# Two heads in one unit of the 64-row chunks of an attention and expert kernel, sums from a column of ones, and a new order

## The chip, the cores and the metric

The kernel runs on one core of a Trainium2 chip. The time is that of one execution on the device, in microseconds. PE is TensorE, PEld its weight load, DVE VectorE, ACT ScalarE, POOL GpSimd, SP SyncE, whose queue issues most of the DMA transfers here.

## What is computed

```python
B, H, S, D = q.shape                      # 4, 8, 576, 64
scores = scale * np.matmul(q, k.transpose(0, 1, 3, 2))
x = (psi_rel / psi_i)[..., None]          # of the two positions alone
h = np.maximum(x @ w1 + b1, 0.0)          # 32 hidden
bias = h @ w2                             # 8 heads
scores = scores + bias.transpose(2, 0, 1)[None, :, :, :]
scores = scores - np.max(scores, axis=-1, keepdims=True)
attn = np.exp(scores)
attn = attn / (np.sum(attn, axis=-1, keepdims=True) + 1e-09)
return np.matmul(attn, v).astype(np.float32)
...
logits = xn @ en.T / tau                  # 2304 tokens, 8 experts, of the attention's output x
expert_idx = np.argmax(logits, axis=1)
gate_w = probs[np.arange(N), expert_idx]
h = np.maximum(x[mask] @ w1[e], 0.0)      # 512 to 1024
out[mask] = gate_w[mask, None] * (h @ w2[e])
```

## The kernel before, in words

The four batches are taken in two pairs `pr`. A chunk (pr, c) with c < 4 holds 128 query rows of each of the two batches; the chunk c = 4 holds the last 64 rows of both. The order is `CHUNKS`: (0, 4), (0, 0) to (0, 3), (1, 0) to (1, 3), (1, 4). A unit (`unit`, L658) is a chunk and a head, 80 in all; units 0 to 7 and 72 to 79 are those of c = 4.

A unit loads its bias `bt` from DRAM (SP, L671), multiplies Q by K on PE (L694, each product as three f16 products), adds the bias and finds the minimum on DVE (L708), takes the exponential on ACT, which also gives the row sums (L711), transposes 128x128 blocks on PE (L725), evicts them to `pts` (ACT or DVE, L731) and multiplies by V on PE (L748). Every second head DVE makes `ri` of the sums (L755, L756) and normalises into `xt` (L762, or L764 for c = 4). A full unit (c < 4) has two batches, whose QK lie in two row tiles of the array (rows 0 to 63 and 64 to 127) and in two PSUM buffers `s0` and `s1`; it has two L708, two L711, nine transposes. A unit of c = 4 has 64 rows of each batch: QK lies in two diagonal tiles (batch b in rows and columns from 64 b on), both write `s0`, and it has one L708, one L711 and five transposes; POOL copies 64 columns of `pp` (L716), so that the last transpose holds both batches.

Beside the units run: `prep_k` (per pair and four heads: raw K in `kr`, of which there is one buffer; the maxima L492 and L494, a transpose L495, L496, L497, the scale and `aq`, L483 to L489; two f16 halves `khl` by ACT and by DVE, L519; ten transposes a head on PE into `s1`, L527, and their eviction `kt`, L530); `prep_q` (L559 and L567 on POOL, L566 on DVE, then a transposing DMA `qt`, L581, since it needs `aq`); and `bias_step` (L583: `hid` on DVE, L617, a product in four column tiles, L632, `stg`, L639 or L643, and a store to DRAM, L654), which makes the bias of a chunk ahead of its units.

When a chunk's eight heads are done, `finish` (L789) normalises the rows, takes logits (L878 to L880), the best expert and gate (L884 to L893) and the rank of each token (L909 to L924). Behind the chunk (1, 3) `early_slots` (L936) fixes the first slots of the experts, behind the last chunk the tokens are gathered and the experts run (`moe`). In units 72 to 79 dummy matmuls of 512 columns (L770) stand between the work of PE.

The order of the work of attention is fixed when the program is built: `Sched` (L123) takes each operation with its engine, an estimated duration and a priority (the unit's number plus an offset such as `oS`, `oB` or `oP`, from the tables at L39 to L97), and lays one fixed row of instructions for each engine. `s1`, `m`, `t0`, `t1` and `o` are one PSUM buffer each; `s1` is shared by QK of batch 1, the K transposes and the dummies.

Of the kernel before, what the change touches and what calls it, by code (L numbers as in the profile page):

```python
# [14 lines left out]
ALU = mybir.AluOpType  # L15
# [35 lines left out]
BBK = 8  # L51
KBS = 12
KA = 19
KB = 27
QA = 13
VA = 39
KLA = 7.607
KLB = 2.85
KHB = 2.886
KP0 = 4.157  # L60
KP1 = 0.138
KH = 2.263
QL1 = 32.538
QL0 = 70.547
BL1 = 14.005
BS1 = 1.189
BP0 = -8.343
PSB = 0
ALPHA = 22.407
# [3 lines left out]
PRLD = 86.205  # L73
AVD, AVD4 = 1315, 732
# [6 lines left out]
PREP = 86.458  # L81
# [182 lines left out]
class Kern:  # L264
# [393 lines left out]
    def unit(self, u):  # L658
# [60 lines left out]
        parts = [("t0", 0, 0, 4, [0])] + ([("t1", 640, 4, 4, [1])] if c < 4 else []) + [("m", 512, 8, 1, [0, 1])]  # L719
# [851 lines left out]
```

## Time and profile before

| | before |
|---|---|
| runs, us | 641.57, 645.21, 650.35 (median 645.21) |
| profiled execution, us | 642.66, its span 640.8 |
| PE busy | 587.6 us (92%) |
| PEld | 397.0 us (62%) |
| DVE | 511.1 us (80%) |
| ACT | 466.9 us (73%) |
| POOL | 159.1 us (25%) |
| mean granted TensorE clock | 0.974 of 2.4 GHz |
| DMA | 119.98 MB, of them 93.43 MB on SP's queue |

Busy shares are means over the whole span. What bounds the kernel differs by stage: the start with the first chunk of 64 rows (0 to 82.8 us), the full chunks (to 348.4), the last chunk of 64 rows (to 373), the gather (to 406), the experts (to 606) and the last scatter.

### The profile page before, as it was taken

The page shows a single profiled execution, that of the slowest core. Times are in us where ns is not written, and L with a number is a line of the kernel's source. Part 1 is how long each engine was busy: PE and PEld are TensorE (multiplying, and loading weights), DVE is VectorE, ACT ScalarE, POOL GpSimd, SP SyncE. Part 2 cuts the span into 40 slices and gives each one's busy share as a digit, 9 for nine tenths or more (in the row PEclk, how much of TensorE's full clock was granted, in tenths as well). Part 3 has the DMA queues.
Part 4 walks back from the last instruction along what each step waited for, and adds up shares of the span by engine and source line. Part 5 has one row for each costly group of instructions (what it writes and reads, how often), then busy time and mean ns, then how long its engine had stood idle before and what let it go on. Part 6 is the DMA issues. An engine that isn't in the chain of part 4 may idle for free.

```text
span 640.8 us, 20769 instructions
## 1 busy us (share of the span) xinstructions
PE 587.6 (92%) x7647; PEld 397.0 (62%) x7647; DVE 511.1 (80%) x1426; ACT 466.9 (73%) x995; POOL 159.1 (25%) x233
## 2 busy tenths in 40 slices
PE   8677899999999889999899988789999999999993
PEld 3233556666877677787787656674576468447741
DVE  8878789899888698888987773887778887987752
ACT  6567679797989798999999543778787667758400
POOL 4454665342021044231202145200000000000173
PEclk9787899999999989999999999899999999999998
DMA  8799988579987948987988459985599479749652
GB/s 186 214 250 206 270 226 187 145 198 229 200 232 98 216 124 164 208 180 176 192 194 182 104 149 304 216 165 144 153 222 230 153 184 216 207 163 208 93 205 97
DMA packets 172027, 119.98 MB, mean 187 GB/s; under 512 B 126327, under 2 KB 147063, under 8 KB 171922
## 3 DMA queue, kind: packets, MB, share of 16 engines
q1 hardware_dynamic: 164706, 93.43, 65.4%
q0 software_dynamic: 7216, 25.14, 13.1%
q8 instruction: 67, 1.10, 0.7%
q14 instruction: 38, 0.31, 0.2%
HBM read 77.24 MB, written 21.87 MB: 155 GB/s over the span
## 4 chain that ended last, share of the span: by engine, by line
issue 35%; PE 30%; DVE 8%; POOL 4%; ACT 4%; DMA 2%; SPq 1%; POOLq 0%; DVEq 0%; ACTq 0%
PE o L748 10%; PE t L725 7%; PE s L694 7%; POOL out L1393 3%; DVE ss L708 2%; DMA macc<-xs,kept 2%; PE m L632 2%; ACT pp L711 1%; PE m L725 1%; DVE khl L519 1%; ACT pts L731 1%; POOL macc L1404 1%; PE s L770 1%; DVE hid L617 1%; DMA kr<-in_k 1%
## 5 line engine op out<-in xcount | busy, mean ns | idle before, releaser
L711 ACT ACTIVATE pp<-ss,mx 128x576 f32<-128x576 f32 x144 | 112.1, 789 | 16.7 <-DVE mx L708 11.7
L708 DVE CUSTOM_DVE_ANT_0 ss<-s,bt 128x576 f32<-128x576 f32 x144 | 104.1, 752 | 15.6 <-PE s L694 13.0
L748 PE MATMUL o<-v,pts 128*64 128x64 f32 x2880 | 103.7, 227 | 0.4 <-DVE xt L762 0.4
L748 PEld LDWEIGHTS o<-v,pts 128*64 128x64 f32 x2880 | 92.5, 140 | 13.9 <-issue 9.0
L1388 PE MATMUL p<-w2s,mht 128*128 (+1 forms) x432 | 97.4, 379 | 0.7 <-DVE macc L1488 0.4
L1388 PE MATMUL p<-w1s,mxt 128*128 (+1 forms) x768 | 96.6, 273 | 0.1
L725 PE MATMUL t<-ident,pp 128*128 128x128 f32 x576 | 85.1, 284 | 3.2 <-ACT pp L711 1.6
L1388 PEld LDWEIGHTS <-mxt 128*128 128x128 f16 (+1 forms) x768 | 73.2, 99 | 17.9 <-issue 2.5
L694 PE MATMUL s<-kt,qt 64*128 64x512 f16 (+3 forms) x960 | 76.4, 285 | 7.2 <-DVE mx L708 3.2
L731 ACT COPY pts<-t 128x512 f32<-128x512 f32 x129 | 71.8, 595 | 13.9 <-PE t L725 11.9
L725 PEld LDWEIGHTS t<-ident,pp 128*128 128x128 f32 x576 | 62.7, 143 | 17.8 <-issue 5.6
L1388 PEld LDWEIGHTS <-mht 128*128 128x128 f16 (+1 forms) x432 | 41.2, 99 | 51.0 <-issue 6.0
L1393 POOL DMA_INDIRECT out<-macc,kept x20 | 19.7, 987 | 206.3 <-DVE macc L1488 206.3
L694 PEld LDWEIGHTS <-qt 64*128 64x128 f16 (+1 forms) x960 | 38.6, 97 | 51.4 <-issue 15.8
L617 DVE TENSOR_SCALAR hid<-L,thr 128x448 f32<-128x448 f32 (+17 forms) x128 | 58.4, 510 | 2.9 <-PE m L632 2.3
L1343 ACT ACTIVATE junk<-raw 128x1024 bf16<-128x1024 f32 x50 | 52.5, 1049 | 6.6 <-DMA raw<-in_moe_w 4.8
L1488 DVE SCALAR_TENSOR_TENSOR macc<-p,aux,macc 128x512 f32<-128x512 f32 x60 | 45.0, 753 | 15.1 <-PE p L1388 9.2
L1450 ACT ACTIVATE h<-p 128x256 f16<-128x256 f32 x72 | 27.1, 381 | 30.6 <-PE p L1388 19.5
L1348 ACT ACTIVATE w1s<-raw,kept 128x1024 f16<-128x1024 f32 x32 | 36.7, 1149 | 13.8 <-DVE kept L1327 13.8
L1349 DVE SCALAR_TENSOR_TENSOR w1s<-raw,kept,w1s 128x1024 f16<-128x1024 f32 x32 | 41.2, 1301 | 0.1
L567 POOL TENSOR_TENSOR qab<-qs,qab 128x512 f16<-128x512 f32 x20 | 24.3, 1215 | 49.9 <-DVE qab L566 27.7
L1451 DVE SCALAR_TENSOR_TENSOR h<-p,h 128x256 f16<-128x256 f32 x72 | 30.0, 421 | 7.4 <-ACT h L1450 6.3
(313 smaller groups left out, 988.1 us busy)
## 6 DMA issues: line engine op xcount, KB each, us to landing
raw<-in_moe_w SPq DMA_DIRECT2D x60, 512.0 KB, 4.6
bt<-bsc SPq DMA_DIRECT2D x64, 288.0 KB, 3.8
bsc<-stg POOLq DMA_DIRECT2D x31, 318.0 KB, 4.0
xs<-row POOLq DMA_DIRECT2D x16, 256.5 KB, 5.9
kr<-in_k SPq DMA_DIRECT2D x32, 128.0 KB, 4.0
v<-in_v SPq DMA_DIRECT2D x32, 128.0 KB, 3.5
q<-in_q SPq DMA_DIRECT2D x8, 512.0 KB, 6.2
bt<-bsc SPq DMA_DIRECT2D x16, 144.0 KB, 3.1
```

What stands on the lines that cost most here:

```text
L617: e.tensor_scalar(hid()[:, 0:N_], self.L[:, 0:N_], self.thr[:, t0 + x:t0 + x + 1], None, ALU.max)
L694: nc.tensor.matmul(out, lq, k, start=xq + xk == 0, stop=xq == 1, tile_position=(64 * b, 0 if c < 4 else 64 * b))
L708: nc.vector.tensor_tensor_reduce(out=sx(), in0=ss[b]()[:, 448 * b:448 * b + S_], in1=bt(), scale=1.0, scalar=3.0e38, op0=ALU.add, op1=ALU. ...
L711: nc.scalar.activation(pp()[:, S_ * b:S_ * b + S_], sx(), AF.Exp, bias=mx()[:, b:b + 1], scale=-1.0, accum_out=sums()[:, h, b:b + 1])
L725: nc.tensor.transpose(t()[:, 128 * k:128 * k + 128], pp()[:, lo + 128 * k:lo + 128 * k + 128], self.ident)
L731: (e.copy if e is nc.scalar else e.tensor_copy)(pts()[:, at:at + n].rearrange("p a b -> p (a b)"), t()[:, 0:128 * n])
L748: nc.tensor.matmul(ob()[r, at:at + 64], pts()[:, 8 if j == 4 else 4 * (b or 0) + j, r], vv[:, 8 + y if j == 4 else 4 * y + j, :], start=j ...
L1343: S.op([("ACT", 1050, lambda: nc.scalar.activation(out() if not own else dst(0), rv() if own else raw(), AF.Square, scale=2.0 ** (-8 if wh ...
L1349: S.op([("DVE", 1192, lambda: nc.vector.scalar_tensor_tensor(dst(1), rv(), zs(), dst(0), ALU.mult, ALU.subtract))], [t + (3,), t + (2,)] + ...
L1388: nc.tensor.matmul(out[c, 0:n], lhs[:, c], w[:, bass.ds(ev[s] + at, n)], start=start, stop=stop)
L1393: ins = nc.gpsimd.indirect_dma_start(self.out, bass.IndirectOffsetOnAxis(ap=self.sidx[:, s:s + 1], axis=0), acc[:, s, :], None, bounds_che ...
L1488: S.op([("DVE", 664, lambda a=a, r=r, p2=p2: v.scalar_tensor_tensor(a, p2(), r, a, ALU.mult, ALU.add))], [("p2", q, s), ("rs", q)], [("acc ...
```

## The change

In a chunk with c = 4 a unit takes two heads (units with an even head; the odd ones return at once), so there are four units a chunk. Its parts:

- QK (L692): 24 matmuls in four tiles; the row tile is the batch, the column tile the head. Batch b goes to `ss[b]`, the two heads to its partitions 0 to 63 and 64 to 127. K of both heads is needed.
- bias and exp run once a batch over 128 partitions; exp no longer accumulates sums. `bt` is loaded in two pieces of 64x576, one a head, instead of three a head. The copy on POOL (L716) is gone. There are nine transposes for the two heads.
- V has a 65th column of ones (a memset on POOL). AV (L743) is 20 matmuls of 65 columns; the 65th gives the sum. `ri` is made from it (L748, L749) behind AV, then the product (L750).
- The dummies (L764) are pairs of 252 columns into `o`, 24 such pairs for 24 matmuls of 512 columns into `s1`. The ones behind the last unit (FO) also wait for the last normalisation.
- All numbers of the tables are new, and so the order of the whole attention part. Line numbers move: L489 is L490, L495 L496, L527 L528, L617 L618, L632 L633, L654 L655, L671 L672, L708 L707, L725 L721, L731 L727, L884 L878.

```diff
-PEN, PACE = 278.345, 2204.15
...
+PEN, PACE = 241.474, 1874.692
...
-        t = self.d["v", pr, hh] = self.buf("v", [128, 4, 10, 64])
+        t = self.d["v", pr, hh] = self.buf("v", [128, 4, 10, D + 1])
 
         def zero():
+            nc.gpsimd.memset(t()[:, :, :, D], 1.0)
...
+        two = c == 4
+        if two and h % 2:
+            return
+        nb, us, end = (1, (u, u + 1), u + 2) if two else (2, (u,), u + 1)
+        p0 = float(u) + (PTW if two else 0)
...
-        ends = [(slice(0, 128), 0, 0, S_)] if c < 4 else [(slice(0, 64), 0, 0, S_), (slice(64, 128), 0, 64, 512), (slice(64, 128), 512, 0, 64)]
...
+        for x, src in enumerate([self.bsc[c][:, at + 640 * y:at + 640 * y + S_] for y in range(2 if two else 1)]):
+            r = slice(64 * x, 64 * x + 64) if two else slice(0, 128)
...
-                            out, lq = ss[0]()[r, col:col + (512 if main else 64)], qt()[r, 4 * xq + h % 4, r]
-                        nc.tensor.matmul(out, lq, k, start=xq + xk == 0, stop=xq == 1, tile_position=(64 * b, 0 if c < 4 else 64 * b))
...
+                        for y, kt in enumerate(kts):
+                            rows, qs = (slice(64 * y, 64 * y + 64), r) if two else (slice(0, 128), slice(0, 128))
+                            k = kt()[r, xk, 0:512] if main else kt()[r, xk, 512 + 64 * b:576 + 64 * b]
+                            nc.tensor.matmul(ss[b]()[rows, col:col + (512 if main else 64)], qt()[r, 4 * xq + h % 4 + y, qs], k, start=xq + xk == 0, stop=xq == 1, tile_position=(64 * b, 64 * y))
...
-        if c == 4:
-            S.op([("POOL", 333, lambda: nc.gpsimd.tensor_copy(pp()[:, 576:640], pp()[:, 512:576]))], [("p", u, 0)], [("p", u, 1)], [pp], p0 + oP)
...
+                        y, to = (x, b) if two else (b, x)
+                        hh, at = (h % 4 + b, k + (D + 1) * b) if two else (h % 4, k + D * b)
+                        n = D + 1 if two else D
...
+        if two:
+            ri = self.buf("ri", [128, 2], pool="sm_ri")
+            S.op([("DVE", 70, lambda: nc.vector.tensor_scalar(ri(), ob()[:, k + D:k + 2 * D + 2:D + 1], 1e-9, None, ALU.add))], [("o", u)], [("ri", u)], [ob, ri], p0 + oX)
+            S.op([("DVE", 75, lambda: nc.vector.reciprocal(ri(), ri()))], [("ri", u)], [("ri", u, 1)], [ri], p0 + oX)
...
-                idle = self.buf("s1", [128, 1024])
...
+                S.op([("PE", 213, lambda: [nc.tensor.matmul(ob()[:, 260:512], self.ones, self.opt[:, 0:4].rearrange("p a b -> p (a b)")[:, 0:252], start=True, stop=True) for _ in range(2)])], [("o", u - 2)], [("fil", 4 * y + (u - 72) // 2)], [ob], p0 + FP)
```

What the new order does shows at three places. First SP in the start, around the loads of K for heads 4 to 7 (`kr`, five pieces a batch; `xs<-opt` clears rows of a table, `bsc` is the bias in DRAM). Before:

```order
L671 DMA bt<-bsc_191 64x576
L671 DMA bt<-bsc_191 64x512
L671 DMA bt<-bsc_191 64x64
L445 DMA kr<-in_k 128x4x64 x4
L448 DMA kr<-in_k 64x4x64
L671 DMA bt<-bsc_191 64x576
L671 DMA bt<-bsc_191 64x512
L671 DMA bt<-bsc_191 64x64
L445 DMA kr<-in_k 128x4x64 x4
L448 DMA kr<-in_k 64x4x64
```

After:

```order
L655 DMA bsc_187<-stg 16x8x636
L672 DMA bt<-bsc_191 64x576 x6
L675 DMA xs<-opt 64x513 x2
L445 DMA kr<-in_k 128x4x64 x4
L448 DMA kr<-in_k 64x4x64
L445 DMA kr<-in_k 128x4x64 x4
L448 DMA kr<-in_k 64x4x64
L331 DMA rcst<-in_rcst 128x309
```

The three loads of `bt` between the two batches of `kr` are gone, and `xs` stands ahead of them instead of behind.

Then PE in the start, around the transpose of the maxima of that K (`m<-ident,kz`; `t<-ident,pp` are the units' transposes, `m<-hid,wt` steps of the bias). Before:

```order
L632 MATMUL m<-hid,wt 32x256 x4
L725 MATMUL t_766<-ident,pp 128x128 x4
L725 MATMUL t_783<-ident,pp 128x128 x4
L748 MATMUL o<-v,pts 64x64 x10
L632 MATMUL m<-hid,wt 32x319 x4
L748 MATMUL o<-v,pts 64x64 x10
L725 MATMUL t_837<-ident,pp 128x128 x4
L495 MATMUL m<-ident,kz 4x128
L725 MATMUL t_860<-ident,pp 128x128 x4
L497 MATMUL m<-ident,kz 128x4
L632 MATMUL m<-hid,wt 32x511 x4
```

After:

```order
L633 MATMUL m<-hid,wt 32x256 x4
L633 MATMUL m<-hid,wt 32x319 x4
L721 MATMUL t_784<-ident,pp 128x128 x4
L721 MATMUL t_792<-ident,pp 128x128 x4
L496 MATMUL m<-ident,kz 4x128
L498 MATMUL m<-ident,kz 128x4
L721 MATMUL m<-ident,pp 128x128
L633 MATMUL m<-hid,wt 32x511 x4
```

The two matmuls of the scale stand ahead of any AV now, and behind two groups of transposes and no longer behind three and two AV.

Last DVE in the tail, where the best expert of the rows of (1, 2) has just been found (`L893 row` is their gate, `s_...` the QK of a unit of c = 4, `mx` the minimum read out, `rjk` the start of the rank). Before:

```order
L893 TENSOR_TENSOR row<-rg,rq 128x2
L708 ISA ss,mx<-s_6977,bt 128x576
L708 ISA mx 128x1
L884 TENSOR_TENSOR lgs<-m,rf 128x16
L885 TENSOR_REDUCE rg<-lgs 128x2
L886 TENSOR_SCALAR rg<-rg 128x2
L860 TENSOR_TENSOR req<-lgs,rg 128x16
L861 TENSOR_TENSOR req<-req,rcst 128x16
L862 TENSOR_REDUCE rg<-req 128x2
L863 TENSOR_TENSOR plan<-req,rg 128x16
```

After:

```order
L887 TENSOR_TENSOR row<-rg,rq 128x2
L727 COPY pts<-m 128x128
L707 ISA ss,mx<-s_6854,bt 128x576
L707 ISA mx 128x1
L707 ISA ss,mx<-s_6857,bt 128x576
L707 ISA mx 128x1
L911 TENSOR_TENSOR rjk<-m,plan 128x16
L912 TENSOR_REDUCE rg<-rjk 128x2
L914 TENSOR_TENSOR rge<-rg,rcst 128x34
```

Where one L708 stood between the two chunks' experts, two follow one another, with an eviction ahead of them, and the rank of the earlier chunk comes ahead of the later chunk's experts.

## Rows read from the trace of the kernel before

**Rows 1.** Windows: per stage length, then busy us (x instructions) by engine, clock, DMA share, GB/s

```profile
0.00:82.80 82.80, 63.58 (x571) 31.90 (x571) 64.94 (x173) 52.45 (x104) 42.21 (x77) 0.88 0.89 227
82.80:200.00 117.20, 114.16 (x1933) 80.99 (x1934) 104.41 (x326) 101.68 (x256) 38.02 (x58) 1.00 0.83 192
200.00:262.00 62.00, 55.23 (x942) 43.79 (x939) 50.89 (x166) 53.09 (x127) 16.27 (x25) 0.97 0.83 173
262.00:348.40 86.40, 84.68 (x1547) 66.80 (x1545) 74.73 (x248) 85.84 (x211) 17.13 (x23) 1.00 0.85 182
348.40:373.00 24.60, 23.29 (x350) 15.16 (x349) 18.68 (x92) 14.36 (x41) 4.08 (x11) 1.00 0.59 148
373.00:406.00 33.00, 26.01 (x280) 19.60 (x277) 18.67 (x76) 14.70 (x22) 21.21 (x22) 1.00 0.78 219
406.00:606.00 200.00, 196.24 (x1886) 128.04 (x1885) 164.19 (x331) 144.81 (x238) 0.41 (x1) 0.99 0.78 181
```

**Rows 2.** Timeline of PE, start: start us, us, line, operation, count [idle before, releaser]

```profile
52.07 0.27 PE L495 MATMUL m<-ident,kz 128*4 128x128 f32 x1
...
66.69 0.93 PE L694 MATMUL s<-kt,qt 64*64 64x512 f16 x12 [2.04 <-DMA qt<-qab]
...
82.83 0.91 PE L694 MATMUL s<-kt,qt 64*128 64x512 f16 x12
```

**Rows 3.** Timeline of DVE, 38 to 58 us: the scale of K, second heads

```profile
43.86 1.49 DVE L492 TENSOR_REDUCE kz<-kr 128x4 f32<-128x1280 f32 x1 [0.49 <-DMA kr<-in_k]
...
45.94 0.16 DVE L494 TENSOR_TENSOR kz<-kz 128x4 f32<-128x4 f32 x1
...
54.78 0.18 DVE L489 RECIPROCAL aq<-kz 128x4 f32<-128x4 f32 x1
```

**Rows 4.** Timeline of SP, 28 to 70 us: DMA issues

```profile
30.68 2.18 SPq L445 DMA_DIRECT2D kr<-in_k  x4
...
33.63 1.97 SPq L671 DMA_DIRECT2D bt<-bsc  x3
35.65 2.59 SPq L445 DMA_DIRECT2D kr<-in_k  x4
...
60.51 2.39 SPq L581 DMA_TRANSPOSE qt<-qab  x1
```

**Rows 5.** Chain that ended last, 338 to 412 us: start us, us to the next, what

```profile
338.70 0.86 PE s L694 x12
...
347.04 1.31 PE o L748 x40
...
349.64 0.50 PE t L725 x4
350.14 0.21 PE s L770
350.35 0.73 PE o L748 x20
...
351.56 0.86 PE s L694 x12
```

**Rows 6.** Timeline of PE, 86 to 89 us: four column tiles

```profile
86.46 0.74 PE L632 MATMUL m<-hid,wt 128*32 128x318 f32 x8
87.14 1.09 PE L725 MATMUL t<-ident,pp 128*128 128x128 f32 x8
```

**Rows 7.** Timeline of DVE, 346 to 376 us: the tail

```profile
359.41 0.17 DVE L884 TENSOR_TENSOR lgs<-m,rf 128x16 f32<-128x16 f32 x1
...
373.40 0.28 DVE L764 TENSOR_TENSOR xt<-o,ri 128x128 f32<-128x128 f32 x1
```

**Rows 8.** Waits of PE, 200 to 262 us: us in total, times, longest us

```profile
PE s L527 <- DVE mx L708: 2.2, 3, 1.1
...
PE s L527 <- ACT kt L530: 0.8, 1, 0.8
```

**Rows 9.** Groups of instructions: busy us, mean ns | idle before, releaser

```profile
L530 ACT COPY kt<-s 128x1280 f16<-128x1280 f16 x16 | 19.6, 1223 | 1.8 <-PE s L527 1.6
```

More of the change, by code (lines that the diff above doesn't have):

```diff
@@ L50 @@
 W1S, W2S, L2P = 3.942, 1.7, 22.604
-BBK = 8
+BBK = 6
 KBS = 12
[L53 to L67, printed above, removed]
+KA = 21
+KB = 35
+QA = 36
+VA = 11
+KLA = 9.369
+KLB = 5.845
+KHB = 0.818
+KP0 = -5.658
+KP1 = -3.883
+KH = 5.81
+QL1 = 9.937
+QL0 = 51.383
+BL1 = 12.618
+BS1 = 1.935
+BP0 = -10.567
 PSB = 0
-ALPHA = 22.407
+ALPHA = 20.886
 ALPHB = 5.392
@@ L90 @@
 XX0 = 2
-STP, STPM = 14.813, 60.738
-VP0 = 123.942
-oL0 = 12.784
+STP, STPM = 12.256, 60.738
+VP0 = 127.364
+oL0 = -2.201
 SZ = {}
@@ L710, in exp @@
             def exp(b=b, sx=sx):
-                nc.scalar.activation(pp()[:, S_ * b:S_ * b + S_], sx(), AF.Exp, bias=mx()[:, b:b + 1], scale=-1.0, accum_out=sums()[:, h, b:b + 1])
-            S.op([("DVE", 677, bias)], [("S", u, b), ("bt", u)], [("ss", u, b)], [ss[b], bt, mx, sx], p0 + oB)
-            S.op([("ACT", 760, exp)], [("ss", u, b)], [("p", u, b)], [mx, sx, pp, sums], p0 + oP)
-        if c == 4:
-            S.op([("POOL", 333, lambda: nc.gpsimd.tensor_copy(pp()[:, 576:640], pp()[:, 512:576]))], [("p", u, 0)], [("p", u, 1)], [pp], p0 + oP)
+                nc.scalar.activation(pp()[:, S_ * b:S_ * b + S_], sx(), AF.Exp, bias=mx()[:, b:b + 1], scale=-1.0, accum_out=None if two else sums()[:, h, b:b + 1])
+            S.op([("DVE", 677, bias)], [("S", u, b), ("bt", u)], [("ss", w, b) for w in us], [ss[b], bt, mx, sx], p0 + oB)
+            S.op([("ACT", 760 if not two else 668, exp)], [("ss", u, b)], [("p", u, b)], [mx, sx, pp] + ([] if two else [sums]), p0 + oP)
         pts = self.buf("pts", [128, 9, 128], pool="pt")
-        parts = [("t0", 0, 0, 4, [0])] + ([("t1", 640, 4, 4, [1])] if c < 4 else []) + [("m", 512, 8, 1, [0, 1])]
+        parts = [("t0", 0, 0, 4, [0]), ("t1", 640, 4, 4, [1]), ("m", 512, 8, 1, [0, 1])]
         for name, lo, at, n, bs in parts:
@@ L737, in unit @@
         ob = self.o
-        k = 128 * (u % 4)
-        to = ("o", u)
+        k = (2 * D + 2) * (u % 4 // 2) if two else 128 * (u % 4)
         def av():
-            vv = v()[:, h % 4]
-            for b in range(2) if c < 4 else (None,):
+            for b in range(2):
                 for j in range(5):
                     for x in range(2):
-                        y, r = x if b is None else b, slice(64 * x, 64 * x + 64)
-                        at = k + 64 * (b or 0)
-                        nc.tensor.matmul(ob()[r, at:at + 64], pts()[:, 8 if j == 4 else 4 * (b or 0) + j, r], vv[:, 8 + y if j == 4 else 4 * y + j, :], start=j == 0, stop=j == 4, tile_position=(0, 64 * x))
@@ L752, in unit @@
             ri = self.buf("ri", [128, 2, 2], pool="sm_ri")
-            rr = lambda: ri()[:, :, 0:nb]
-            sm = lambda: sums()[:, h - 1:h + 1, 0:nb]
-            S.op([("DVE", 70, lambda: nc.vector.tensor_scalar(rr(), sm(), 1e-9, None, ALU.add))], [("p", u, b) for b in range(nb)], [("ri", u)], [sums, ri], p0 + oX)
-            S.op([("DVE", 75, lambda: nc.vector.reciprocal(rr(), rr()))], [("ri", u)], [("ri", u, 1)], [ri], p0 + oX)
+            S.op([("DVE", 70, lambda: nc.vector.tensor_scalar(ri(), sums()[:, h - 1:h + 1], 1e-9, None, ALU.add))], [("p", u, b) for b in range(2)], [("ri", u)], [sums, ri], p0 + oX)
@@ L758, in norm @@
+            S.op([("DVE", 75, lambda: nc.vector.reciprocal(ri(), ri()))], [("ri", u)], [("ri", u, 1)], [ri], p0 + oX)
             def norm():
@@ L760, in norm @@
                 xo = xt().rearrange("p b (h d) -> p h b d", d=64)[:, h - 1:h + 1]
[L761 to L772 removed]
+                nc.vector.tensor_tensor(xo, xb, ri().unsqueeze(3).to_broadcast([128, 2, 2, 64]), ALU.mult)
+            S.op([("DVE", 335, norm)], [("ri", u, 1), ("o", u - 1), ("o", u)], [("x", pr, c), ("x", pr, c, h // 2)], [ob, ri, xt], p0 + oX)
+        if u > 71:
+            for y in range(2 * FN):
+                S.op([("PE", 213, lambda: [nc.tensor.matmul(ob()[:, 260:512], self.ones, self.opt[:, 0:4].rearrange("p a b -> p (a b)")[:, 0:252], start=True, stop=True) for _ in range(2)])], [("o", u - 2)], [("fil", 4 * y + (u - 72) // 2)], [ob], p0 + FP)
+        if end == len(UNITS):
+            S.op([("NONE", 1, self.open_moe)], [("o", x) for x in range(u - 15, end)] + [("fil", x) for x in range(8 * FN)] + [("wp", 2, 0, e, 0) for e in range(PRE)], ["open"], [], p0)
             for s in range(EA):
```

73 lines of the change are left out of this document (29 added, 44 removed).

## The prediction

> **What bounds the kernel now.** I read the profiled run by stages first, then the start, the middle and the tail by engine. The stages [rows 1] have PE busy 97% of 82.8 to 200 us, 98% of 262 to 348.4 and 98% of 406 to 606, so a stage that starts earlier there ends earlier by as much. Three stages are not PE's: the start (63.58 us of 82.80), the stretch 200 to 262 (55.23 of 62.00), where the K of the second batch pair is prepared, and 373 to 406, where the last rows are routed and gathered. The changed chunks, with c = 4, lie in the start (units 0 to 7) and in 348.4 to 373 (units 72 to 79); there PE is busy too, 23.29 us of 24.60, but part of that is dummy matmuls (L770).
>
> In the start the path is the K of heads 4 to 7. SP issues the second batch's part at 35.65, behind three loads of `bt` [rows 4]; DVE takes its maximum at 43.86 (after 0.49 us of waiting for it), combines at 45.94 and has the scale `aq` at 54.78 + 0.18 [rows 3]; in between PE takes the transpose that the scale needs only at 52.07, six microseconds after it was ready. `qt` is issued at 60.51 [rows 4], the QK of unit 4 starts at 66.69 after 2.04 us for it, and the first unit of a full chunk (unit 8) at 82.83 [rows 2].
>
> In the tail the path passes to DVE: from the logits of chunk (1, 2), L884 at 359.41, to the last normalisation, 373.40 + 0.28 [rows 7], DVE stands idle for less than 1 us. The last AV of a full chunk ends at 347.04 + 1.31 = 348.35 [rows 5]. In what follows t counts from 348.35.
>
> **What a pair costs on PE.** Two heads before: QK 2 x 0.86, transposes 2 x (0.50 + 0.11), AV 2 x 0.73 [rows 5], 4.4 us. A pair now:
> - QK: 24 matmuls in four tiles. If the column tiles run side by side, it is the 12 steps of a full unit's QK, 0.86; I take 1.0, since weights are loaded twice as often. The nearest row for column tiles is L632: four column tiles, 8 matmuls of 128x318, are done 0.68 us after they begin (86.46 to 87.14) [rows 6]; a dummy of 512 columns takes 0.21 [rows 5], so at that rate 8 x 318 columns one after another would take 1.04. If nothing overlaps, a pair is 2 x 0.86 = 1.72.
> - Nine transposes, 9 x 0.125 = 1.1 (4 take 0.50).
> - AV: 20 matmuls of 65 columns, half of the 40 of 64 in a full unit (1.31 [rows 5]); but 20 took 0.73 before for one head, so half of a full unit is about 0.7 and a pair has twice 10 matmuls of 0.067. A pair costs between 0.75 and 1.46; I take 1.33, near the upper, since the tile's columns grow.
>
> So 3.4 for 4.4, 1.0 us a pair: 4 us in the start, hidden under its waits, and 4 us in the tail.
>
> The Trainium skill (TensorE: Matmul & The Clock Gate, Part 3: Packing small matmuls) speaks against the full overlap: it says that a weight load overlaps a running matmul only where the row group differs, and here neighbours in issue order, the two heads, share one. L632, whose four tiles share all rows, overlaps nevertheless [rows 6]; by the rule QK is 1.72 (rival b), by the row about 1.0.
>
> **Other edits.** DVE: as many passes of L708 (two a pair, one a head before), as many small operations, but the add and the reciprocal of the sums now read AV's result and stand behind it: about 0.35 us behind the last AV, which was hidden before since the sums came from exp; it is inside the tail's sum below. ACT loses 8 evictions of 128 columns and the sums' readouts, and waits for DVE there anyway: nothing gained. POOL loses 16 copies off the path. Loads: 48 issues of `bt` become 16. POOL's column of ones in `v` is set once a buffer, long before use. The dummy matmuls keep their columns.
>
> **Start: -5.5 us (-9 to -2).** With fewer `bt` issues SP issues the ten loads of that K one behind the other; without the three `bt` (33.63 to 35.60 [rows 4]) the second part goes out 2.0 us sooner, so the combination at 45.94 comes at about 43.5 [rows 3]. On PE the transpose now stands behind two groups of transposes and ahead of the first AV, on DVE fewer rows of `hid` stand between the scale and the lower halves of K. Walking the new order with the durations above, `aq` comes at about 51 (54.96 before), the QK of the third pair at about 60.5 (66.69) and unit 8 at 74 to 77 (82.83). I take 77.3: the later end, since the new order moves work of the bias before it and QK now needs both `s` buffers. Lower bound -9 (unit 8 at 74), upper -2 (the load alone). The next stage is 97% PE, so this passes through; what is late next is unit 8's own bias, not K.
>
> **Middle: 0 (-4 to +4).** Between unit 8 and the last full AV PE has two QK of pairs for three QK of heads (-0.6), a few fewer transposes and one dummy (-0.4), and a bias step more, moved out of the start (8 matmuls, 0.85). The K transposes of the second half of the batch pair wait for `s1` three times, 2.2 us [rows 8]; they stand in another order now, `kr` of heads 4 to 7 is loaded about two units earlier, but the last four transposes are packed behind one another with an eviction of 1.22 us each between [rows 9] on the one `s1`. PE idles 6.77 us in 200 to 262 [rows 1]; I see neither half nor twice of it with confidence: 0, with -4 (most of that idle gone) and +4 (four evictions exposed).
>
> **Tail: -3.7 us (-6 to -1.5).** Before, the DVE stretch from the logits of (1, 2) to the last normalisation runs from t = 11.06 to 25.33, 14.3 us. After, PE has ahead of these logits one QK (1.0), nine transposes (1.1), 14 half dummies (14 x 0.105 = 1.5) and one AV (1.3), 4.9, then 24 logits matmuls (0.6): they are ready at 5.5 instead of 10.5 or so. The DVE stretch holds the same chains, one normalisation more (0.28 + 0.35), one eviction (0.27), and the add and reciprocal of the others (0.35): 14.3 + 1.25 = 15.6; with some 0.5 us of waiting for the last pair's transposes and AV it ends at 21.6, against 25.33. So -3.7. Lower bound -6: no lengthening and no waits (5.5 us off at the front); upper -1.5: pairs have only half as many units in flight, so that each of the last two waits once for QK, bias, exp, transposes, eviction and AV in a row (about 1 us each). The dispatch behind it starts earlier by as much, and 406 to 606 only shifts.
>
> Sum: 642.66 - 5.5 + 0 - 3.7 = 633.5 for the profiled run, whose span is 640.8. The median of the runs, 645.21, is 2.5 above it (641.57 to 650.35), so 633.5 to 636.0; I say 635.
>
> **Rivals.**
> a) More: the waits of 200 to 262 shrink too. For it: PE idles 6.77 us there [rows 1], K comes two units earlier. Against it: the packed transposes. Half of that idle and the start's -9 give 642.66 - 9 - 3.5 - 4 = 626.
> b) The four tiles do not overlap (or the change is hidden anyway). QK of a pair 1.72: PE costs 0.7 more a pair, about 2.8 in the tail's four pairs, so that the tail gives -1, the start -2 to -5: 638 to 641. For it: tiles in one row group, and before two diagonal tiles did 6 matmuls each in 0.86, as long as a full unit with twice the output rows, so a tile of 64 rows costs a whole one. Against it: L632 [rows 6].
> c) Slower: QK now fills `s0` and `s1`, and the transposes of K use `s1` too, which had been free for them in the start (heads wrote `s0` alone). From the QK of one pair to that of the next the chain is QK, bias of batch 1 (0.75), K's transposes (0.6), eviction (1.22 [rows 9]), twice over for the two heads: four handoffs of about 4.5 us. There is room from about 55 to 82.83; it decides where unit 8 comes behind 87 us, that is if all handoffs add 4 us and aq doesn't gain. Then +5 in the start, -2 left in the tail, +2 in the middle: 648.
>
> **Chances.** Forecast 0.55, (a) 0.22, (b) 0.15, (c) 0.08. A measurement of this kernel tells about 2%, 12.9 us, from no change: faster 0.27 ((a), and 0.05 of the forecast's lower end), slower 0.04 (half of (c)), the rest within. Range 626 to 643: it takes in (a)'s 626 and (b); half of (a)'s cases and (c) stay outside.
>
> **What would show it.** Right: unit 8's QK at 74 to 78, `aq` at about 51; a pair's QK of about 1.0 us; last normalisation 21 to 22 us behind the last full AV's end (25.33 before); 406 to 606 as long as before. Wrong: a QK of 1.7 us in the tail (b); K transposes waiting for `s1` or for L708 in the start (c); the stretch of the second K with PE idle clearly below 5 us (a) or above 9.

## The result and the profile after

| | before | after |
|---|---|---|
| median of 13 runs each, us | 645.21 | 639.35 (635.90 to 641.12) |
| ratio to before, 95% interval | | 0.9905 (0.9879 to 0.9931) |
| profiled execution, us (span) | 642.66 (640.8) | 637.61 (635.8) |

The kernel became faster by about 1%, 6 us; 10 were forecast, and the time lies inside the forecast range. On a second chip the same kernel was measured again beside others (e10 below): 0.9887 (0.9861 to 0.9913).

The page of the profile after, its parts on the span and the engines (busy us, share of the span, instructions):

```profile
span 635.8 us, 20690 instructions
PE 581.2 (91%) x7663; PEld 394.0 (62%) x7663; DVE 510.9 (80%) x1422; ACT 465.4 (73%) x975; POOL 151.9 (24%) x221
```

PE lost 6.4 us of work, DVE none, ACT 1.5. The stages after (windows: length, then busy us by engine, clock, DMA share, GB/s), cut where the same work ends as in [rows 1]:

```profile
0.00:76.50 76.50, 56.97 (x559) 28.36 (x559) 67.25 (x166) 49.62 (x91) 35.48 (x68) 0.89 0.89 220
76.50:115.00 38.50, 35.17 (x485) 20.89 (x484) 34.16 (x97) 29.17 (x72) 17.99 (x29) 0.96 0.66 165
...
200.00:262.00 62.00, 54.27 (x901) 41.56 (x900) 48.71 (x154) 54.95 (x125) 15.24 (x23) 0.97 0.92 171
...
346.60:368.00 21.40, 19.21 (x361) 16.01 (x362) 18.03 (x89) 13.34 (x35) 2.88 (x5) 1.00 0.45 125
368.00:401.50 33.50, 28.53 (x275) 20.73 (x274) 17.88 (x79) 15.16 (x22) 22.27 (x22) 0.92 0.82 211
```

Two stages show what happened: 76.5 to 115, where PE is busy for 35.17 us of 38.50 at a clock of 0.96, though [rows 1] had 97% at 1.00 there, and 346.6 to 368, three microseconds shorter than the stage of 24.60 before.

The same places in both kernels give the difference by stages. The mark of a unit is its first L708 (L707 after) on DVE. Unit 8 before (timeline of DVE: start us, us, instruction):

```profile
84.13 0.75 DVE L708 CUSTOM_DVE_ANT_0 ss<-s,bt 128x576 f32<-128x576 f32 x1
```

Unit 16 before (the same view):

```profile
114.95 0.76 DVE L708 CUSTOM_DVE_ANT_0 ss<-s,bt 128x576 f32<-128x576 f32 x1
```

Unit 8 after:

```profile
77.69 0.75 DVE L707 CUSTOM_DVE_ANT_0 ss<-s,bt 128x576 f32<-128x576 f32 x1
```

Unit 16 after:

```profile
115.16 0.74 DVE L707 CUSTOM_DVE_ANT_0 ss<-s,bt 128x576 f32<-128x576 f32 x1
```

So unit 8 came 6.4 us earlier, and unit 16 no earlier at all. Unit 17 is 2.1 us earlier again (119.53 for 121.63): some work that stood behind unit 16's mark stands ahead of it now. For all stages, from the marks of both traces (the first normalisation of 128x256 behind the last full AV ends "units 16 to 71", the end of the last normalisation ends "tail", the first w1 matmul of the experts ends "gather"):

| stage | before, us | after, us | difference | forecast |
|---|---|---|---|---|
| start, to unit 8 | 84.13 | 77.69 | -6.4 | -5.5 |
| units 8 to 15 | 30.82 | 37.47 | +6.7 | part of the middle, 0 |
| units 16 to 71 | 233.45 | 231.46 | -2.0 | part of the middle, 0 |
| tail | 25.28 | 20.89 | -4.4 | -3.7 |
| gather | 32.12 | 33.33 | +1.2 | 0 |
| experts to the end | 235.0 | 235.0 | 0 | 0 |
| span | 640.8 | 635.8 | -5.0 | -9.2 |

### The profile page after: what moved, and what is told of

Same layout as the page of the kernel before. It is cut to its first block, busy times and chain, and to the rows that moved or that the text cites. A ratio compares the mean times of both kernels' runs of the same rounds, so it can differ in the third digit from the quotient of the medians.

```text
span 635.8 us, 20690 instructions
## 1 busy us (share of the span) xinstructions
PE 581.2 (91%) x7663; PEld 394.0 (62%) x7663; DVE 510.9 (80%) x1422; ACT 465.4 (73%) x975; POOL 151.9 (24%) x221
## 4 chain that ended last, share of the span: by engine, by line
PE 37%; issue 35%; DVE 7%; POOL 5%; DMA 3%; ACT 2%; SPq 1%; POOLq 0%; DVEq 0%; ACTq 0%
PE o L743 12%; PE t L721 9%; PE s L692 7%; POOL out L1387 3%; PE m L633 3%; DVE hid L618 2%; PE m L721 2%; DVE ss L707 2%; DMA macc<-xs,kept 2%; DMA kr<-in_k 1%; DVE khl L520 1%; POOL macc L1398 1%; PE o L764 1%; PE e L1046 1%; PE s L528 1%
## 5 line engine op out<-in xcount | busy, mean ns | idle before, releaser
L707 DVE CUSTOM_DVE_ANT_0 ss<-s,bt 128x576 f32<-128x576 f32 x144 | 103.7, 752 | 13.0 <-PE s L692 9.1
L743 PE MATMUL o<-v,pts 128*64 128x64 f32 (+1 forms) x2880 | 101.2, 226 | 2.0 <-DVE xt L750 1.1
L743 PEld LDWEIGHTS o<-v,pts 128*64 128x64 f32 x2880 | 91.2, 139 | 14.6 <-issue 7.5
L721 PE MATMUL t<-ident,pp 128*128 128x128 f32 x576 | 85.1, 283 | 4.5 <-ACT pp L710 4.4
L727 ACT COPY pts<-t 128x512 f32<-128x512 f32 x135 | 74.6, 590 | 8.1 <-PE t L721 3.7
L721 PEld LDWEIGHTS t<-ident,pp 128*128 128x128 f32 x576 | 62.5, 142 | 18.5 <-ACT pp L710 8.6
L692 PE MATMUL s<-kt,qt 64*128 64x512 f16 (+3 forms) x960 | 69.1, 285 | 4.4 <-DVE mx L707 2.8
L618 DVE TENSOR_SCALAR hid<-L,thr 128x448 f32<-128x448 f32 (+17 forms) x128 | 61.5, 531 | 5.2 <-PE m L633 4.3
L692 PEld LDWEIGHTS <-qt 64*128 64x128 f16 (+1 forms) x960 | 33.9, 97 | 44.6 <-issue 17.2
L1444 ACT ACTIVATE h<-p 128x256 f16<-128x256 f32 x72 | 27.1, 382 | 30.5 <-PE p L1382 18.8
L633 PE MATMUL m<-hid,wt 128*32 128x256 f32 (+16 forms) x240 | 32.7, 547 | 8.7 <-ACT pts L727 3.0
```

Of the source, the lines that this page charges most:

```text
L618: e.tensor_scalar(hid()[:, 0:N_], self.L[:, 0:N_], self.thr[:, t0 + x:t0 + x + 1], None, ALU.max)
L633: nc.tensor.matmul(m()[32 * x:32 * x + 32, 0:n], w(x), hx[x]()[:, a:a + n], start=True, stop=True, tile_position=(0, 32 * x))
L692: nc.tensor.matmul(ss[b]()[rows, col:col + (512 if main else 64)], qt()[r, 4 * xq + h % 4 + y, qs], k, start=xq + xk == 0, stop=xq == 1, t ...
L707: nc.vector.tensor_tensor_reduce(out=sx(), in0=ss[b]()[:, 448 * b:448 * b + S_], in1=bt(), scale=1.0, scalar=3.0e38, op0=ALU.add, op1=ALU. ...
L721: nc.tensor.transpose(t()[:, 128 * k:128 * k + 128], pp()[:, lo + 128 * k:lo + 128 * k + 128], self.ident)
L727: (e.copy if e is nc.scalar else e.tensor_copy)(pts()[:, at:at + n].rearrange("p a b -> p (a b)"), t()[:, 0:128 * n])
```

## The start and the tail after

In the start the chain of K moved in the way that was forecast. DVE after (timeline), the rows that answer to [rows 3]:

```profile
42.47 1.49 DVE L493 TENSOR_REDUCE kz<-kr 128x4 f32<-128x1280 f32 x1 [0.96 <-DMA xs<-opt]
...
44.27 0.15 DVE L495 TENSOR_TENSOR kz<-kz 128x4 f32<-128x4 f32 x1
...
50.24 0.18 DVE L490 RECIPROCAL aq<-kz 128x4 f32<-128x4 f32 x1
```

SP after (timeline), to [rows 4]:

```profile
34.69 3.06 SPq L445 DMA_DIRECT2D kr<-in_k  x4
...
53.94 2.33 SPq L582 DMA_TRANSPOSE qt<-qab  x1
```

The combination of the maxima is 1.7 us earlier (44.27 for 45.94), `aq` 4.5 (50.24 for 54.78), the issue of `qt` 6.6 (53.94 for 60.51). The second part of K itself was issued only 1.0 us sooner (34.69 for 35.65), where 2.0 were forecast.

The start varies from one execution to the next: the same changed kernel has unit 8's mark at 77.69 here and at 79.31 in e10.

The tail on PE, from the chain that ended last (start us, us to the next, what), answers to [rows 5]:

```profile
345.26 1.32 PE o L743 x40
346.57 0.86 PE s L692 x24
347.44 1.02 PE t L721 x8
348.46 0.11 PE m L721
348.57 1.29 PE o L764 x12
349.86 1.32 PE o L743 x40
```

A QK of 24 matmuls takes 0.86 us, as long as the 12 of one head or of a full unit; the second head is free. An AV of a pair takes 1.32 for 2 x 0.73, nine transposes 1.13 for 2 x 0.61. A pair costs 3.31 us where two heads cost 4.40.

## The experiments

Each is described by its edit, the expectation on record, and what it gave. In the tables "8 to 15" is the time from unit 8's mark to unit 16's.

**e1 and e2, the change and its order apart.** e1 is the changed kernel with the old numbers, e2 the kernel before with the new ones. From the numbers `Sched` lays the rows of each engine anew, so e1's order is not that of before row for row, nor e2's that of after:

```diff
 e1, on after:
-PEN, PACE = 241.474, 1874.692
+PEN, PACE = 278.345, 2204.15
...
 e2, on before:
-PEN, PACE = 278.345, 2204.15
+PEN, PACE = 241.474, 1874.692
...
```

> The changed kernel with the old numbers of the tables (only the two the new code needs, AVD and PTW, are new): two heads a unit, but the old priorities. Theory A (the pairs save PE time in the tail, the new order saves the start): unit 8's QK stays near 82, the tail from the last full AV to the last normalisation is 2 to 4 us shorter than 25.3, total about 641 to 643. Rival B (the new order does it all): 645 or more. Rival C (the pairs do it all, the order nothing): 638 to 640.

> The kernel before with the new numbers of the tables: one head a unit in the chunks of 64 rows, new priorities. Theory A: K of heads 4 to 7 comes earlier, unit 8's QK 2 to 4 us before 82.83, which is given back in units 8 to 15; the tail as before, 25 us; total 643 to 647. Rival B: 638 to 640. Rival C: 645 to 650, since the numbers were chosen for pairs.

| | ratio to before | start | 8 to 15 | 16 to 71 | tail | gather | span |
|---|---|---|---|---|---|---|---|
| e1, pairs, old numbers | 1.0182 (1.0134 to 1.0230) | 81.96 | 39.34 | 241.41 | 21.90 | 36.76 | 659.9 |
| e2, heads, new numbers | 1.0092 (1.0055 to 1.0128) | 84.98 | 27.91 | 238.04 | 25.08 | 31.03 | 646.5 |

No theory had both: B expected e1, C nearly e2. Each half alone makes the kernel slower, by 12 and by 6 us. What the tail shows is clean nevertheless. It takes 20.9 and 21.9 us with pairs, 25.3 and 25.1 without, whatever the order: the tail's gain of 3.4 to 4.4 us belongs to the pairs. The start's gain needs both, and the traces show why. In e1 the loads of K follow one another, and the maxima are combined at 45.85, but PE takes their transpose only 6.3 us later (6.1 before; PE of e1, timeline):

```profile
52.12 0.27 PE L496 MATMUL m<-ident,kz 128*4 128x128 f32 x1
```

In e2 the transpose comes 0.5 us behind the combination, but three loads of `bt` a head stand between the loads of K again, and the combination is late (timelines of DVE and of PE):

```profile
49.42 0.16 DVE L494 TENSOR_TENSOR kz<-kz 128x4 f32<-128x4 f32 x1
49.95 0.27 PE L495 MATMUL m<-ident,kz 128*4 128x128 f32 x1 [3.56 <-ACT stg L639]
```

So `aq` comes at 54.67 in e1, 52.64 in e2, and 50.24 with both.

e1's profiled execution is the slowest of its five (662.17 us, the median is 657.51). It loses 8.5 us in units 8 to 15, 8.0 in units 16 to 71, 4.6 in the gather and the rest behind it. Part of the 8.5 is work that its order puts there: 320 matmuls of AV for 200. In units 16 to 71 PE waits in the preparation of the second K (us in total, times, longest us; 215 to 262 us):

```profile
PE t L721 <- ACT pp L710: 4.3, 3, 3.8
PE s L528 <- DVE khl L520: 2.5, 2, 2.3
...
```

With two more (2.0 and 1.8) these waits are 10.6 us, beside a lower clock (0.87 in 200 to 262), against 6.77 us of idle in 200 to 262 before [rows 1]. Where e2 loses in units 16 to 71 was not traced further.

**e3 and e4, less work on DVE in the start.** These were meant for the units 8 to 15, but the bias steps of chunk (0, 1), which they cut, lie in the start in the changed kernel; the steps between units 8 and 16 are those of chunk (0, 2). So they answer another question.

```diff
-                e.tensor_scalar(hid()[:, 0:N_], self.L[:, 0:N_], self.thr[:, t0 + x:t0 + x + 1], None, ALU.max)
+                None if c == 1 and x else e.tensor_scalar(hid()[:, 0:N_], self.L[:, 0:N_], self.thr[:, t0 + x:t0 + x + 1], None, ALU.max)
...
-                    nc.tensor.matmul(m()[32 * x:32 * x + 32, 0:n], w(x), hx[x]()[:, a:a + n], start=True, stop=True, tile_position=(0, 32 * x))
+                    nc.tensor.matmul(m()[32 * x:32 * x + 32, 0:n], w(x), hx[0 if c == 1 else x]()[:, a:a + n], start=True, stop=True, tile_position=(0, 32 * x))
```

> The changed kernel, in the same order on every engine, without three of the four hidden rows in the bias steps of chunk (0, 1) (24 of the 32 L618 of that chunk; the products read the first row four times): it leaves out part of that chunk's bias. Theory D (DVE is full in units 8 to 15, so what the start wins is given back there): with 11 us less on DVE the QK of unit 16 comes 4 us or more ahead of 113.9 (114.1 in the changed kernel), total 634 to 636. Rival E (the loss is the one stall of PE at 107 to 109 us, behind ACT's eviction, and the lower clock after it): QK of unit 16 at 112 to 114, total 638 to 640.

> The kernel before with the same rows of hid left out in the bias steps of chunk (0, 1), as a control: it leaves out part of that chunk's bias. PE is busy 97% there, so by theory D, and by E, 644 to 646, unchanged within 1 us; if it gains as much as the changed kernel does (3 us or more), DVE bounded these units before too, and what was given back has another cause.

| | ratio to before | start | 8 to 15 | span |
|---|---|---|---|---|
| e3, after | 0.9827 (0.9760 to 0.9894) | 77.74 | 37.35 | 636.6 |
| e4, before | 0.9966 (0.9933 to 1.0000) | 79.49 | 30.81 | 637.1 |

The start of e3 (window 0 to 77 us, DVE is the third engine):

```profile
0.00:77.00 77.00, 58.03 (x563) 29.33 (x565) 57.88 (x144) 49.92 (x92) 36.27 (x70) 0.84 0.88 220
```

The same window of the changed kernel:

```profile
0.00:77.00 77.00, 57.47 (x565) 28.59 (x567) 67.75 (x168) 50.12 (x92) 35.98 (x68) 0.89 0.88 218
```

The ratio of e3 is lower than the changed kernel's, but the intervals overlap, and the profiled spans are within 1 us. Ten microseconds less of DVE work, and unit 8 comes at 77.74 for 77.69 (79.31 in e10): in the changed kernel DVE doesn't bound the start. In the kernel before it bounded part of it, behind `aq` (54.10 in e4 for 54.78): there the same cut brings unit 8 from 84.13 to 79.49. In e6, which has the start of before, it comes at 82.32, so the gain is 2.8 to 4.6 us. And e4's trace shows that a lead at unit 8 does pass through before: 4.6 us earlier at unit 8, 4.7 at unit 16 (110.30 for 114.95). So the forecast's step holds in the old order; something in the new one's units 8 to 15 takes the lead away. What reaches the end is less: this execution of e4 is the fastest of ten (638.89 us), and their median, 644.07, is 1.2 us below that of before beside it.

**e5 and e6, less work on DVE in units 8 to 15.** The same edit with `c == 2`.

> The changed kernel in the same order, without three of the four hidden rows in the bias steps of chunk (0, 2) instead of (0, 1): these are the steps whose L618 stand in units 8 to 15 (it leaves out part of that chunk's bias). Theory D (DVE is full between units 8 and 16, so the start's lead is given back to it): the QK of unit 16 comes 3 us or more ahead of 114.1, total 635 to 637. Rival E (the lead is lost to PE's own waits behind ACT near 107 us and the lower clock after them): QK of unit 16 at 113 to 114, PE at half its clock at 110 to 112 as before, total 638 to 640.

> The kernel before with the same rows left out in chunk (0, 2), as control (it leaves out part of that chunk's bias): PE is busy 96% between units 8 and 16 there, so by theory D unit 16's QK gains at most 1.5 us of its 113.9 relative to unit 8's, total 643 to 645. If it gains 3 us or more, DVE bounded these units before as well.

What they gave stands in the table behind e12.

**e7, the wait behind ACT.** At 107 us PE of the changed kernel waits. PE of the changed kernel there (timeline):

```profile
106.27 0.91 PE L692 MATMUL s<-kt,qt 64*128 64x512 f16 x12
108.41 0.33 PE L721 MATMUL m<-ident,pp 128*128 128x128 f32 x1 [1.23 <-ACT stg L640]
109.09 0.33 PE L721 MATMUL m<-ident,pp 128*128 128x128 f32 x1 [0.36 <-ACT pts L727]
109.35 2.17 PE L743 MATMUL o<-v,pts 128*64 128x64 f32 x40
111.45 1.72 PE L633 MATMUL m<-hid,wt 128*32 128x447 f32 x8
...
114.13 0.91 PE L692 MATMUL s<-kt,qt 64*128 64x512 f16 x12
```

ACT of the changed kernel there (timeline):

```profile
106.44 1.07 ACT L727 COPY pts<-t 128x512 f32<-128x512 f32 x2 [2.47 <-PE o L743]
107.40 0.96 ACT L640 ACTIVATE stg<-m,corr 128x254 f32<-128x254 f32 x2
```

The engines and the clock of the changed kernel around it (windows, columns as above):

```profile
90.00:95.00 5.00, 4.75 (x34) 2.27 (x35) 5.00 (x10) 3.31 (x8) 3.46 (x6) 1.00 0.62 136
95.00:100.00 5.00, 4.47 (x94) 3.02 (x93) 5.00 (x17) 3.82 (x11) 1.44 (x3) 1.00 0.78 192
...
108.00:110.00 2.00, 1.24 (x18) 0.93 (x20) 1.00 (x4) 1.58 (x5) 0.55 (x1) 0.92 0.89 104
110.00:112.00 2.00, 2.00 (x34) 1.54 (x34) 0.60 (x2) 2.00 (x6) 0.00 (x0) 0.50 0.85 210
112.00:114.00 2.00, 2.00 (x16) 0.86 (x8) 0.81 (x3) 0.72 (x3) 0.57 (x1) 0.73 0.40 135
```

The transpose at 108.41 writes `m`, which still holds a bias step; ACT evicts that (L640) at 107.40, since it stands behind two evictions into `pts` (106.44) that waited 2.47 us for the AV that reads the old `pts`. PE idles 1.23 and 0.36 us, and then the granted clock is 0.50 (1.2 GHz) from 110 to 112 and 0.73 to 114: the AV takes 2.17 us for 1.39, the bias step 1.72. The edit gives `pts` a third buffer, and leaves every row of the order as it is:

```diff
-                    self.p[n] = P(n, k)
+                    self.p[n] = P(n, 3 if n == "pt" else k)
```

> The changed kernel in the same order with a third buffer behind pts (the planner still counts two): ACT's eviction at 106.4 us no longer waits for the AV that reads the old pts, so the eviction of stg behind it and PE's wait of 1.2 us for it go. Rival E: PE's wait at 107 us goes, the clock stays at 1.00, QK of unit 16 2 to 3 us earlier than 114.1, total 636 to 638. Theory D: the wait goes but DVE is full, QK of unit 16 at 113 to 114.2, total 638.5 to 640.

**e10, e11, e12.** e10 is the changed kernel once more, e11 is e7 once more on the same chip, e12 has the edits of e5 and of e7.

> The changed kernel again, beside e11 on one chip: a second profile shows whether PE's wait near 107 us and the granted clock of 0.50 behind it belong to the kernel (theory E: both there again, QK of unit 16 about 37.5 us behind unit 8's) or to one execution (clock 1.00, 36 us or less). Ratio to before 0.988 to 0.993.

> The third buffer of pts again: by theory E no wait and no drop near 107 us, unit 16's QK 34.5 to 35.5 us behind unit 8's, ratio to before 0.984 to 0.989, 1.5 to 3 us below e10. If it is within 0.5 us of e10, what is won at 107 us is lost later.

> The third buffer of pts and the rows of hid left out in chunk (0, 2) together (it leaves out part of that chunk's bias). If the two causes, PE's wait with the lower clock and the full DVE, make up what is lost between units 8 and 16, these eight units take 30.5 to 32 us (37.5 in the changed kernel, 34.6 with the third buffer alone, 33.6 with the rows left out alone, 30.8 before). If the two are one and the same loss, 33 to 34.5 us. Total 632 to 636, since the gathers in front of the experts hold part of an earlier arrival.

| | ratio to before | start | 8 to 15 | 16 to 71 | tail | gather | span |
|---|---|---|---|---|---|---|---|
| after | 0.9905 (0.9879 to 0.9931) | 77.69 | 37.47 | 231.46 | 20.89 | 33.33 | 635.8 |
| e10, the same | 0.9887 (0.9861 to 0.9913) | 79.31 | 37.33 | 232.25 | 20.89 | 33.03 | 636.8 |
| e7, third `pts` | 0.9887 (0.9859 to 0.9915) | 77.93 | 34.50 | 231.87 | 20.91 | 31.09 | 634.6 |
| e11, third `pts` | 0.9900 (0.9868 to 0.9932) | 78.66 | 34.68 | 232.15 | 20.92 | 31.07 | 635.1 |
| e5, less `hid` | 0.9818 (0.9790 to 0.9845) | 78.57 | 33.58 | 231.25 | 20.88 | 31.24 | 633.8 |
| e12, both | 0.9811 (0.9750 to 0.9872) | 78.72 | 32.28 | 232.24 | 20.91 | 30.59 | 633.6 |
| e6, before, less `hid` | 0.9953 (0.9920 to 0.9985) | 82.32 | 29.22 | 235.69 | 25.29 | 31.66 | 640.4 |

PE at that place with the third buffer (e11, timeline):

```profile
107.30 0.91 PE L692 MATMUL s<-kt,qt 64*128 64x512 f16 x12
108.14 0.33 PE L721 MATMUL m<-ident,pp 128*128 128x128 f32 x1
108.83 0.33 PE L721 MATMUL m<-ident,pp 128*128 128x128 f32 x1 [0.36 <-ACT pts L727]
109.08 1.39 PE L743 MATMUL o<-v,pts 128*64 128x64 f32 x40
...
112.31 0.91 PE L692 MATMUL s<-kt,qt 64*128 64x512 f16 x12
```

PE with less `hid` (e5, timeline):

```profile
104.90 0.91 PE L692 MATMUL s<-kt,qt 64*128 64x512 f16 x12
107.04 0.33 PE L721 MATMUL m<-ident,pp 128*128 128x128 f32 x1 [1.23 <-ACT stg L640]
107.72 0.33 PE L721 MATMUL m<-ident,pp 128*128 128x128 f32 x1 [0.36 <-ACT pts L727]
107.98 1.39 PE L743 MATMUL o<-v,pts 128*64 128x64 f32 x40
...
111.21 0.91 PE L692 MATMUL s<-kt,qt 64*128 64x512 f16 x12
```

Both theories were partly right, and these rows give the sizes. From the QK at 106.27 to the next at 114.13 the changed kernel takes 7.86 us (both starts are in the trace of PE), e5, which has the same waits but keeps its clock, 6.31, e11, which has neither the wait of 1.23 nor the drop (that of 0.36 stays), 5.01. So the lower clock cost 1.55 us and the wait 1.30. e5 gained 3.9 us in the eight units; less the clock's 1.55, leaving out `hid` is worth 2.3. The sum, 1.30 + 1.55 + 2.3 = 5.2, is what e12 gained (37.47 to 32.28, just above the 30.5 to 32 of the first theory).

But the 2.3 are not all the new order's. Before, the same cut (e6) gained 1.6 us, so DVE had little slack there either; the new order puts four more L618 into these units (32 for 28), and DVE is busy for all of 90 to 100 us. About 0.8 is what DVE costs more than before. The counterpart of e12 is e6, and against it the eight units are still 3.1 us longer (32.28 for 29.22). Most of that is PE's work that moved there. AV from unit 8's QK to unit 16's (window with L748 alone: length, PE, PEld, clock, DMA share, GB/s), before:

```profile
82.83:113.91 31.08, 7.15 (x200) 6.32 (x200) 1.00 0.85 197
```

After (L743 alone):

```profile
76.54:114.13 37.59, 9.10 (x240) 8.22 (x240) 0.95 0.68 169
```

That is six AV of 1.32 for four and two of one head, 1.2 us more, and a bias step more (72 matmuls for 64, about 0.85): 2.1 us. The AV comes from later units (2354 of its matmuls behind for 2394), the bias step from the start (200 for 208), as the forecast had it. So of the 6.7 us the wait is 1.30, the clock 1.55, the work moved there 2.1 and DVE's load about 0.8; about 1.0 was not traced.

e10 shows the wait and the drop again (0.50 from 112 to 114), and so does e3 (0.50 from 110 to 112), so they belong to the order. But e11 is not below e10 as a whole (0.9900 and 0.9887, the intervals overlap), and e7 was only 1.6 us below the first median: a third buffer behind `pts` is no version that beats the changed kernel for certain. Its 2.7 us in the eight units (with 0.7 of an earlier unit 8) reach the end of the tail, 366.41 for 369.78, and the first expert matmul, 397.48 for 402.81; of these 5.3 us between e10 and e11 the span keeps 1.7. The waits of PE between 390 and 420 us in e10:

```profile
PE st L1315 <- ACT junk L1337: 3.2, 3, 1.8
```

In e11 (the same view):

```profile
PE p L1406 <- DMA macc<-xs,kept: 1.7, 2, 1.3
PE st L1315 <- DVE mxt L1411: 1.3, 1, 1.3
```

The earlier arrival waits for the gathered rows (1.7 us) and for the copy behind them (1.3), which e10 doesn't; the rest of what is given back was not traced. It is so in every trace with an early tail: from the last normalisation to the end the kernel takes 267.1 us before, 267.0 in e10 and 268.3 in the changed kernel's first trace, but 268.7 to 269.5 in e11, e7, e5 and e12, where the tail ends at 364.2 to 366.4.

**e8 and e9, the dummies of the tail.** On e7's kernel, without the twelve matmuls at 348.57, and without all 48 (there `range(0)`):

```diff
-                S.op([("PE", 213, lambda: [nc.tensor.matmul(ob()[:, 260:512], self.ones, self.opt[:, 0:4].rearrange("p a b -> p (a b)")[:, 0:252], start=True, stop=True) for _ in range(2)])], [("o", u - 2)], [("fil", 4 * y + (u - 72) // 2)], [ob], p0 + FP)
+                S.op([("PE", 213, lambda: [nc.tensor.matmul(ob()[:, 260:512], self.ones, self.opt[:, 0:4].rearrange("p a b -> p (a b)")[:, 0:252], start=True, stop=True) for _ in range(0 if u == 72 else 2)])], [("o", u - 2)], [("fil", 4 * y + (u - 72) // 2)], [ob], p0 + FP)
```

> The kernel with the third buffer of pts (e7), without the twelve dummy matmuls ahead of the first AV of the last chunk (1.29 us on the chain of the changed kernel, 348.57 to 349.86). Theory F (the tail is a DVE stretch that starts when the logits of chunk (1, 2) are there): the last normalisation comes 1.0 to 1.3 us earlier behind the last full AV than 20.9, total 636 to 637. Rival G (something else holds the logits or the stretch's later waits swallow it): within 0.3 us of 20.9, total 637.5 to 638.

> The same without any of the 48 dummy matmuls of the last chunk (10 us at 0.21 us a pair is not on the path, only about 1.6 us ahead of the DVE stretch). Theory F with the clock held: last normalisation 1.3 to 1.6 us earlier, total 635.5 to 637. Rival H (PE idles in the tail and the granted clock falls to 0.50 in the tail or the gather): QK and AV of the last pairs take twice as long somewhere, total 638 to 642.

These two ran on a chip on which the kernel before takes 658.37 us; only ratios and stretches can be compared. e8: 0.9880 (0.9841 to 0.9920), tail 20.90 us; e9: 0.9930 (0.9899 to 0.9961), tail 21.75. In e8 PE reaches the logits and waits (timeline of PE):

```profile
351.23 0.17 PE L872 MATMUL m<-ent,xtt 128*128 128x8 f16 x1 [0.95 <-ACT pts L727]
```

In e9 the clock falls (windows of the tail):

```profile
360.00:365.00 5.00, 2.31 (x48) 1.60 (x45) 4.38 (x27) 1.78 (x9) 1.07 (x2) 0.87 0.69 258
365.00:370.00 5.00, 3.75 (x58) 3.19 (x59) 3.21 (x20) 0.27 (x2) 0.12 (x1) 0.50 0.02 5
```

Theory F fell: with the dummies gone the logits start at 351.23 for 351.33 in the changed kernel, since `m` is evicted by ACT behind the normalisation of chunk (1, 3), and DVE comes to them at 352.55 for 352.45. The 1.29 us of dummies on the chain hide under that. Without any (e9) the clock is 0.81 to 0.87 from 350 to 365 and falls to 0.50 in 365 to 370, and the last AV is late (2.43 us for 1.39): the rival H, for 0.85 us of tail, and the gather behind it takes 45.9 us for 42.5 in e8.

## Why the prediction was right, and where its sum was not

- **Start.** Right, a little more than forecast: unit 8's QK at 76.54 (82.83 before, 77.3 taken; 78.09 in e10), by the steps named: the K loads without `bt` between, the early transpose, `aq` at 50.4 (50.24 + 0.18). e1 and e2 show that neither step does it alone. The loads gave half of what was taken (1.0 us for 2.0), the transpose made up for it. What the forecast did not see: in the kernel before DVE's work held part of the start (e4), in the new order less of it gains nothing (e3).
- **"The next stage is 97% PE, so this passes through"** is the step that failed, and with it "Middle: 0 (-4 to +4)", whose two stretches came to +6.7 and -2.0, together +4.7, outside its own bounds. That the stage is full on PE is true of the order before, and e4 shows that there a lead passes. In the new order the stage has a wait behind ACT (1.30), the clock after it (1.55), a fuller DVE (about 0.8, e12's gain over e11 less e6's), 2.1 of PE's work moved in, and about 1.0 that was not traced. Of the 2.1 the bias step (0.85) was in the forecast; the AV comes from later units, and 1.3 of the -2.0 of units 16 to 71 is its coming back. The forecast had counted PE's work between unit 8 and the last full unit, but not what eight units hold, nor DVE's load in them.
- **The sum.** Middle and gather cost 5.9 us that were put at 0; start and tail gave 1.6 more than forecast. That the time lies in the range all the same is owed to these and to a range wide enough for rivals (a) and (b): the forecast itself, 635, is 4.4 us off, of a gain of 10.
- **Tail.** Right in mechanism and nearly in size: -4.4 for -3.7. The logits were done at t = 5.5 as forecast (352.08, behind 346.57), the DVE stretch took 15.1 us (352.45 to 367.51) for 15.6. A pair's QK was 0.86 for the 1.0 taken, AV 1.32 for 1.33, transposes 1.13 for 1.1. The AV came out by luck: the forecast set 20 matmuls against the 40 of a full unit, but the trace has 40 for a pair as well, so that a full unit's 1.31 was the row to take. The work of dummies ahead of the logits, 1.5 us of that sum, was hidden by ACT (e8): the size came out, one term of it was not what held the time.
- **Rival b** is refuted: a pair's QK takes 0.86 us, not 1.72. The Trainium skill (TensorE: Matmul & The Clock Gate, Part 3: Packing small matmuls) lets a weight load overlap a running matmul only where the row group differs. The trace differs: neighbours of one row group, the two heads, cost nothing, 24 matmuls in the 0.86 us of 12.
- **Rival a** did not come: PE idles 7.73 us in 200 to 262, 6.77 before [rows 1]. **Rival c** neither: PE waits around the K transposes in the start, 0.66, 0.43 and 0.98 us, but unit 8 is early. Its fear, a lead lost to waits for shared PSUM, came in another place, for `m` behind ACT.
- **Gather.** +1.2 us, not in the forecast: the granted clock was 0.59 in 382 to 386 us in this execution, behind 1.34 us of waiting for a gather. It was low there in e10 too (0.87 and 0.70 from 382 to 390), and 1.00 in e3, e5, e7 and e11 with the same order, where the gather takes 31.1 to 31.3 us; why was not tried.

## What to carry to other kernels

A stage that one engine fills at 97% passes on an earlier start only as long as its own work and order stay; when the order is made anew, count each engine's work in the first few units behind the place that gets earlier, and look for evictions that share a buffer with the engine that bounds. Packing small matmuls into unused column tiles saved PE time at once and by the amount counted, but with the numbers made for the old units it made this kernel slower: with a static order the new durations need a new order, and the two have to be measured together. A buffer's wait of 1.3 us cost 2.85 here, since the granted clock fell behind it; in e5 the same wait came without the fall.

## What the runs showed of the hardware

- Four tiles of 64x64, loaded and used in turn, took 0.86 us for 24 matmuls, as long as two tiles with 12; two diagonal tiles that wrote the same columns of one PSUM buffer had cost the same 0.86. In the changed kernel's trace the loads for the second matmul of each of the four tiles run from 346.53 to 346.65 us, between its first matmul (from 346.50) and its second (from 346.74).
- PE idle for 1.23 and 0.36 us was followed by a granted clock of 0.50 (1.2 GHz) in the changed kernel, in e10 and in e3, while in e5 the same two waits were followed by 1.00. The idle time at the place alone does not decide; what does was not found.
